# Norm statistics of two token blocks in one interleaved pass, with a retuned static schedule

## The chip, the cores and the metric

The kernel runs on one core of one Trainium2 chip. The metric is the device time of one execution in microseconds (us), lower is better. Every ratio below is of runs taken in the same rounds on the same chip.

## The reference, cut to what matters

```python
def _layernorm(x, axis=-1, eps=1e-05):
    m = jnp.mean(x, axis=axis, keepdims=True)
    v = jnp.var(x, axis=axis, keepdims=True)
    return (x - m) / jnp.sqrt(v + eps)

# x: (B, T, D) = (2, 4000, 144), 4 heads of 36
h = _layernorm(x); x = x + 0.5 * (_silu(h @ w_ff1a) @ w_ff1b)
h = _layernorm(x); q, k, v = split_heads(h @ w_qkv)          # cut
p = softmax(q @ k.T * 36 ** -0.5); x = x + (p @ v) @ w_o      # cut
h = _layernorm(x); ... # gated unit, depthwise convolution of 5 taps, silu, projection (cut)
h = _layernorm(x); x = x + 0.5 * (_silu(h @ w_ff2a) @ w_ff2b)
return _layernorm(x)
```

There are five layer norms over rows of 144 features. 8000 tokens are 64 blocks of 125 rows, so 320 block norms. The large part is the attention: 4000 x 4000 scores for each of 4 heads and 2 batches, each of which needs an exponential.

## The kernel before

The kernel is a program that writes a program. Python generators (one for each norm, projection, score tile) ask a scheduler for an engine; the scheduler keeps an assumed clock for each engine, takes the next step by assumed cost and by a *policy*, and the result is a fixed order of instructions for each engine with semaphore waits worked out from data dependences. Every instruction is issued from one helper line, so the profile gives all of them one line number (L169) and groups have to be told apart by tile.

The norm before, for `n` blocks of 125 rows (`c` is a chunk of four blocks):

```python
for j in range(n):                              # one block each: 144 columns -> 6 numbers
    op("dve", "bn_stats", ST[0:rows, u, j, :], X[0:rows, c * NB + b0 + j, :], ..., cost=0.21)
...
for j in range(n):                              # merge the even and odd halves -> mean, variance
    op("dve", "bn_aggr", MV[0:rows, u, j, :], ST[0:rows, u, j, :], ..., cost=0.08)
calm = mode["front"] or mode["tail"]
op("dve" if calm else "pool", "tensor_scalar", RS[.., 1, ..], MV[0:rows, u, 0:n, 1], LN_EPS, None, op0=ALU.add, ...)
op("pool", "tensor_tensor", RS[.., 0, ..], RS[.., 1, ..], NHALF[..], op=ALU.pow, ...)   # 1/sqrt
# middle: four POOL passes XN = (X - mean) * rstd, cost=XN_COST
# tail:   on ACT (activation Identity with scale and bias tiles, cost=c_act(D)) or on DVE
```

A score tile is 128 x 1000 exponentials. ACT does most of them. DVE does some by integer arithmetic: two reads of PSUM (128x500 each), then five passes over a 128x1000 tile of 16-bit numbers in SBUF. The policy decides which:

```python
BASE = dict(AHEAD=0.56, DSLACK=1.0, DGAP=3.5, OFREE=1, OBATCH=0, LATE=0.3, BMIN=2.2, SOON=3, LIVE=2, MAXQ=3, EARLY=1)
POLICY = {...}     # the same names, with one value for each of 18 phases of the attention (cut)

# a tile goes to DVE only if (cut)
live_dve[0] < now("LIVE") and early[0] < now("EARLY") and ... \
    and R.free["dve"] < R.free["pe"] + now("DSLACK") and R.free["pe"] > last_dve[0] + now("DGAP")
```

The other names set how the remaining matmuls and the post-processing (output projection, convolution, second feed-forward) are mixed in between.

The softmax here doesn't subtract the row's maximum and nothing guards it: scores larger than these inputs give would overflow.

Of the kernel before, what the change touches and what calls it, by code (L numbers as in the profile page):

```python
# [6 lines left out]
ALU = mybir.AluOpType  # L7
BF16 = mybir.dt.bfloat16
F16 = mybir.dt.float16
F32 = mybir.dt.float32  # L10
U16 = mybir.dt.uint16

D = 144
# [9 lines left out]
NB = 4  # L23
# [296 lines left out]
def bass_standalone__conformer_family_zipformer__speech_kernel(  # L320
# [28 lines left out]
    def sb(name, shape, dt=BF16):  # L349
        return nc.alloc_sbuf_tensor(name, [128] + list(shape), dt)  # L350
# [2 lines left out]
    NPT = 9  # L353
    NU = 5
    NAN = 5
    BASE = dict(AHEAD=0.56, DSLACK=1.0, DGAP=3.5, OFREE=1, OBATCH=0, LATE=0.3, BMIN=2.2, SOON=3, LIVE=2, MAXQ=3, EARLY=1)
    POLICY = {
        "AHEAD": [0.56, 0.56, 0.56, 0.56, 0.56, 0.75, 0.75, 0.56, 0.56, 0.56, 0.56, 0.56, 0.6, 0.56, 0.56, 0.56, 0.56, 0.56],
        "DGAP": [3.5, 3.5, 3.5, 3.5, 3.5, 3.5, 3.5, 3.5, 3.5, 3.5, 3.5, 3.5, 3.5, 3.5, 3.5, 3.5, 3.5, 4.0],
        "OFREE": [1, 1, 1, 1, 1, 1, 1, 1, 1, 1, 1, 1, 1, 1, 2, 1, 1, 1],  # L360
        "LATE": [0.3, 0.3, 0.6, 0.3, 0.3, 0.3, 0.3, 0.3, 0.3, 0.3, 0.3, 0.3, 0.3, 0.3, 0.3, 0.3, 0.3, 0.3],
        "BMIN": [2.2, 2.2, 2.2, 2.2, 2.2, 2.2, 2.2, 2.2, 2.2, 2.2, 2.2, 2.2, 2.2, 2.2, 2.2, 1.8, 1.8, 2.2],
        "MAXQ": [3, 3, 3, 3, 3, 3, 2, 2, 3, 3, 3, 3, 3, 3, 3, 3, 3, 3],
    }
    ROT = 0
    SPLIT = 0
# [17 lines left out]
    VG = 7  # L384
    X = sb("X", [NBLK, D])
    XN = sb("XN", [NXN, NB, D])
    ST = sb("ST", [NXN, NB, 6], F32)
    MV = sb("MV", [NXN, NB, 2], F32)
    RS = sb("RS", [NXN, 3, NB], F32)
    NHALF = sb("NHALF", [NB], F32)  # L390
    DUM = sb("DUM", [1], F32)
# [82 lines left out]
    for c in range(CPB, NCH):  # L474
        load_x("sp", c)

    op("pool", "memset", MV[:, :, :, :], 0.0, w=[("MV", u) for u in range(NXN)])
    op("act", "activation", DUM[:, :], NHALF[:, 0:1], ACT.Silu, bias=0.0, scale=1.0, r=["NHALF"], w=["DUM"], cost=1.6)
    for WE, WB, nm, eng in ((WE1, WB1, "W1", "dve"), (WE2, WB2, "W2", "pool")):
        op(eng, "memset", WE[0:HD, :, 0:64], 0.0, w=[(nm, "a", 2)], cost=0.15)  # L480
# [109 lines left out]
    def ln(c, bs, e=False):  # L590
        n, b0, rows = len(bs), bs[0], TB + e
        xe = ["XE"] * e
        u = yield need("dve", xnp)
        for j in range(n):
            op("dve", "bn_stats", ST[0:rows, u, j, :], X[0:rows, c * NB + b0 + j, :], r=[("X", c, b0 + j)] + xe,
               w=[("ST", u, j)], cost=0.21)
        yield need("dve", hold=mode["front"] or mode["tail"])
        for j in range(n):
            op("dve", "bn_aggr", MV[0:rows, u, j, :], ST[0:rows, u, j, :], r=[("ST", u, j)], w=[("MV", u)], cost=0.08)
        calm = mode["front"] or mode["tail"]  # L600
        if not calm:
            yield need("pool")
        op("dve" if calm else "pool", "tensor_scalar", RS[0:rows, u, 1, 0:n], MV[0:rows, u, 0:n, 1], LN_EPS, None,
           op0=ALU.add, r=[("MV", u)], w=[("VE", u)], cost=0.08 if calm else 0.25)
        if calm:
            yield need("pool")
        op("pool", "tensor_tensor", RS[0:rows, u, 0, 0:n], RS[0:rows, u, 1, 0:n], NHALF[0:rows, 0:n], op=ALU.pow,
           r=[("VE", u), "NHALF"], w=[("RS", u)], cost=0.7 if calm else POW_COST)
        if not calm:
            op("pool", "tensor_scalar", RS[0:rows, u, 2, 0:n], MV[0:rows, u, 0:n, 0], -1.0, None, op0=ALU.mult,  # L610
               r=[("MV", u)], w=[("NM", u)], cost=0.3)
            for j in range(n):
                op("pool", "tensor_scalar", XN[0:rows, u, j, :], X[0:rows, c * NB + b0 + j, :], RS[0:rows, u, 2, j:j + 1],
                   RS[0:rows, u, 0, j:j + 1], op0=ALU.add, op1=ALU.mult,
                   r=[("X", c, b0 + j), ("NM", u), ("RS", u)] + xe, w=[("XN", u)], cost=XN_COST, lat=XN_LAT)
        elif mode["tail"] and R.free["act"] + XSLACK < R.free["dve"]:
            yield need("dve", hold=True)
            op("dve", "scalar_tensor_tensor", out=RS[0:rows, u, 2, 0:n], in0=MV[0:rows, u, 0:n, 0], scalar=-1.0,
               in1=RS[0:rows, u, 0, 0:n], op0=ALU.mult, op1=ALU.mult, r=[("MV", u), ("RS", u)], w=[("NM", u)], cost=0.08)
            yield need("act")  # L620
            for j in range(n):
                op("act", "activation", XN[0:rows, u, j, :], X[0:rows, c * NB + b0 + j, :], ACT.Identity,
                   bias=RS[0:rows, u, 2, j:j + 1], scale=RS[0:rows, u, 0, j:j + 1],
                   r=[("X", c, b0 + j), ("NM", u), ("RS", u)] + xe, w=[("XN", u)], cost=c_act(D))
        else:
            yield need("dve")
            for j in range(n):
                op("dve", "tensor_scalar", XN[0:rows, u, j, :], X[0:rows, c * NB + b0 + j, :], MV[0:rows, u, j, 0:1],
                   RS[0:rows, u, 0, j:j + 1], op0=ALU.subtract, op1=ALU.mult,
                   r=[("X", c, b0 + j), ("MV", u), ("RS", u)] + xe, w=[("XN", u)], cost=0.231)  # L630
        return u

    XSLACK = 0.0
    XN_COST = 0.5
    XN_LAT = 0.5
    POW_COST = 1.1

    def ln_tr(c, s, bs, e=False):
        u = yield from ln(c, bs, e)
# [950 lines left out]
```

## Time and profile before

| | |
|---|---|
| time, median of the runs first taken | 954.24 us (954.09 to 955.26) |
| profiled span, mean granted clock | 953.0 us, 0.997 |
| last exponential tile done | 919.8 us |
| tiles on ACT and on DVE (128x1000) | 863 and 129 |

One place it did not look at is shown here. The first fence is PE's part of the timeline of the kernel before (start, duration, engine, operation, tiles, shape, count, and in brackets the idle time before it with what ended it); the second is the table of busy time by stretch (window, length, PE, PE weight load, DVE, ACT, POOL, then granted clock, DMA share, GB/s) around the same moment.

```profile
637.95 0.38 PE L169 MATMUL PS<-PT,VA 64*37 64x500 bf16 x4
640.37 0.39 PE L169 MATMUL PS<-U,DG 128*128 128x500 bf16 x1 [2.04 <-POOL U L169]
```

```profile
640.00:642.00 2.00, 1.63 (x11) 0.37 (x11) 1.51 (x3) 0.78 (x1) 0.31 (x2) 0.72 0.00 0
642.00:644.00 2.00, 2.00 (x16) 0.42 (x14) 1.00 (x2) 1.12 (x2) 0.00 (x0) 0.50 0.00 0
```

PE ran nothing for 2.04 us before a small POOL copy was done (tile U, the edges that the convolution borrows from its neighbour chunk; the copy itself stood behind four normalising passes that took 3.31 us), and then ran at half clock (0.50) for 3.4 us, from 640.87 to 644.28 us by windows of 0.1 us. The row of clock in tenths that the prediction read averages over 24 us a slice and hides it.

### The profile page before, as it was taken

Reading aid. Unit: us, or ns where it says so; the run is one execution under the profiler, and the core shown is the slowest. Engines: PE = TensorE matmul, PEld = TensorE weight load, DVE = VectorE, ACT = ScalarE, POOL = GpSimd, SP = SyncE. Lnnn points to the kernel's source line nnn. Section 1 sums busy time; section 2 is a strip of 40 time slices with the busy share of each in tenths; the row PEclk is TensorE's granted clock in tenths of the full one; section 3 lists DMA queues with packets and bytes.
Section 4 is the critical chain, followed back from the end, with each engine's and each line's share of the span. In section 5 each row is a group of like instructions: output and inputs, shape, how many; then the busy total and the mean of one; then the engine's idle time right before and its main releaser. Section 6 shows DMA issues by size and latency. Waiting matters only on the chain.

```text
span 953.0 us, 27142 instructions
## 1 busy us (share of the span) xinstructions
PE 902.5 (95%) x11491; PEld 407.6 (43%) x11491; DVE 861.2 (90%) x2291; ACT 904.9 (95%) x1150; POOL 308.3 (32%) x535
## 2 busy tenths in 40 slices
PE   8899999999999999999999999989998999999996
PEld 7543433443343444434444433433343344434456
DVE  7997797999999897899999999998989899999885
ACT  5799999999999999999999999999999999999984
POOL 4220024513134333333225421531234143431452
PEclk9999999999999999999999999999999999999999
DMA  4000000000000000000000000000000000000000
GB/s 120 23 2 2 2 2 2 1 2 1 2 2 1 2 2 2 7 1 2 2 8 7 3 8 2 13 1 2 2 14 1 1 9 1 14 1 3 7 8 20
DMA packets 7195, 7.34 MB, mean 8 GB/s; under 512 B 2372, under 2 KB 7074, under 8 KB 7074
## 3 DMA queue, kind: packets, MB, share of 16 engines
q1 hardware_dynamic: 5916, 5.14, 1.8%
q8 instruction: 90, 1.47, 0.7%
q10 hardware_dynamic: 1158, 0.48, 0.2%
q14 instruction: 31, 0.25, 0.1%
HBM read 3.31 MB, written 2.30 MB: 6 GB/s over the span
## 4 chain that ended last, share of the span: by engine, by line
ACT 43%; PE 34%; DVE 18%; POOL 3%; issue 1%; DMA 0%; POOLq 0%; DVEq 0%
ACT PT L169 37%; PE PS L169 34%; DVE PT L169 9%; ACT TH L169 5%; DVE HT L169 2%; POOL XN L169 2%; DVE ST L169 1%; POOL RS L169 1%; DVE XT L169 1%; DVE OTF L169 1%; DVE X L169 1%; DVE MV L169 1%; DVE AN L169 0%; DMA X<-in_x_dram 0%; DVE XN L169 0%
## 5 line engine op out<-in xcount | busy, mean ns | idle before, releaser
L169 ACT ACTIVATE PT<-PS 128x1000 bf16<-128x1000 f32 (+1 forms) x879 | 812.9, 1047 | 13.1 <-PE PS L169 11.3
L169 PE MATMUL PS<-QT,KT 64*64 64x500 bf16 x3968 | 412.5, 385 | 22.5 <-ACT PT L169 14.9
L169 PE MATMUL PS<-PT,VA 64*37 64x500 bf16 x3968 | 362.0, 375 | 4.5 <-DVE OTF L169 1.8
L169 PEld LDWEIGHTS PS<-QT,KT 64*64 64x64 bf16 x3968 | 123.7, 104 | 219.1 <-ACT PT L169 140.0
L169 DVE TENSOR_SCALAR PT<-PS 128x500 uint16<-128x500 f32 x258 | 172.4, 669 | 16.2 <-PE PS L169 15.1
L169 POOL TENSOR_SCALAR RS<-MV 125x4 f32<-125x4 f32 x118 | 39.8, 337 | 438.0 <-DVE MV L169 432.6
L169 DVE TENSOR_TENSOR PT<-PT 128x1000 uint16<-128x1000 uint16 (+1 forms) x258 | 174.0, 679 | 1.9
L169 PEld LDWEIGHTS PS<-PT,VA 64*37 64x37 bf16 x3968 | 114.6, 95 | 111.8 <-issue 30.5
L169 DVE TENSOR_SCALAR PT<-PT 128x1000 uint16<-128x1000 uint16 (+1 forms) x387 | 157.1, 422 | 2.3
L169 POOL TENSOR_SCALAR XN<-X,RS 125x144 bf16<-125x144 bf16 x236 | 153.9, 664 | 6.1
L169 POOL TENSOR_TENSOR RS<-RS,NHALF 125x4 f32<-125x4 f32 (+2 forms) x99 | 97.9, 994 | 118.2 <-DVE RS L169 113.3
L169 ACT ACTIVATE TH<-PS 128x500 bf16<-128x500 f32 (+2 forms) x208 | 111.6, 558 | 9.2 <-PE PS L169 8.4
L169 DVE SCALAR_TENSOR_TENSOR HT<-TH,PS 128x500 bf16<-128x500 bf16 (+1 forms) x145 | 87.0, 615 | 14.8 <-ACT TH L169 14.6
L169 DVE SCALAR_TENSOR_TENSOR X<-PS,X 125x288 bf16<-125x288 f32 x128 | 57.4, 452 | 23.0 <-PE PS L169 21.5
L169 DVE BATCH_NORM_STATS2 ST<-X 125x6 f32<-125x144 bf16 (+1 forms) x320 | 75.3, 294 | 1.3 <-DMA X<-in_x_dram 1.1
L169 PE MATMUL PS<-XT,WA 72*128 72x500 bf16 (+2 forms) x272 | 74.1, 366 | 2.0 <-ACT XTQ L169 0.9
L169 PE MATMUL PS<-WB,HT 128*125 128x144 bf16 (+1 forms) x640 | 52.6, 230 | 0.4 <-DVE HT L169 0.3
L169 PEld LDWEIGHTS PS<-WB,HT 128*125 128x125 bf16 (+1 forms) x640 | 44.1, 136 | 14.1 <-issue 6.3
L169 PE MATMUL PS<-IDENT,XN 125*72 125x125 bf16 x512 | 43.0, 222 | 5.3 <-POOL XN L169 1.8
L169 DVE COPY XT<-PS 72x1000 bf16<-72x1000 bf16 (+1 forms) x64 | 39.7, 623 | 5.9 <-PE PS L169 5.6
L169 PEld LDWEIGHTS PS<-IDENT,XN 125*72 125x72 bf16 x512 | 31.3, 112 | 25.9 <-issue 11.5
L169 POOL COPY U<-U 128x2 bf16<-128x2 bf16 (+1 forms) x54 | 13.8, 279 | 78.2 <-DVE U L169 78.2
(90 smaller groups left out, 636.0 us busy)
## 6 DMA issues: line engine op xcount, KB each, us to landing
X<-in_x_dram SPq DMA_DIRECT2D x16, 140.6 KB
out_dram<-XN SPq DMA_DIRECT2D x14, 140.6 KB
WA<-in_w_ff1a_dram ACTq DMA_DIRECT2D x1, 144.0 KB
WB<-in_w_ff1b_dram ACTq DMA_DIRECT2D x1, 144.0 KB, 2.5
WA<-in_w_ff2a_dram SPq DMA_DIRECT2D x1, 144.0 KB
WB<-in_w_ff2b_dram SPq DMA_DIRECT2D x1, 144.0 KB
out_dram<-XN SPq DMA_DIRECT2D x2, 70.3 KB
out_dram<-XN SPq DMA_DIRECT2D x1, 139.5 KB
```

The lines of the kernel that those rows point to most:

```text
L169: ins = getattr(eng, o.name)(*o.a, **o.k)
```

## The change

Intent: the instruction that takes statistics gives six numbers a row (125x6 from 125x144 in the trace of the kernel before), and a second one merges them to two (125x2 from 125x6). The change takes the six to be those of the even and of the odd columns, separately. If two blocks are read alternately, x0[0], y0[0], x0[1], y0[1], ..., the even half *is* one block and the odd half the other. One instruction of 288 columns then replaces two of 144 and both merges. Of a half's three numbers the change takes one as the mean and one as the sum of squared deviations, so the add of epsilon also divides by 144. At the same time the policy was retuned and the assumed POOL costs were raised. The core of the diff, cuts marked:

```diff
-    BASE = dict(AHEAD=0.56, DSLACK=1.0, DGAP=3.5, OFREE=1, OBATCH=0, LATE=0.3, BMIN=2.2, SOON=3, LIVE=2, MAXQ=3, EARLY=1)
+    BASE = dict(AHEAD=0.56, DSLACK=0.2, DGAP=4.0, OFREE=1, OBATCH=1, LATE=0.3, BMIN=2.0, SOON=2, LIVE=3, MAXQ=3, EARLY=2)
     POLICY = {   # (all lists by phase replaced; cut)
-    ST = sb("ST", [NXN, NB, 6], F32)
-    MV = sb("MV", [NXN, NB, 2], F32)
+    ST = sb("ST", [NXN, NB, 3], F32)
-    op("pool", "memset", MV[:, :, :, :], 0.0, w=[("MV", u) for u in range(NXN)])
-        for j in range(n):
-            op("dve", "bn_stats", ST[0:rows, u, j, :], X[0:rows, c * NB + b0 + j, :], r=[("X", c, b0 + j)] + xe,
-               w=[("ST", u, j)], cost=0.21)
-        yield need("dve", hold=mode["front"] or mode["tail"])
-        for j in range(n):
-            op("dve", "bn_aggr", MV[0:rows, u, j, :], ST[0:rows, u, j, :], r=[("ST", u, j)], w=[("MV", u)], cost=0.08)
+        for j in range(0, n, 2):
+            op("dve", "bn_stats", ST[0:rows, u, j:j + 2, :].rearrange("p i k -> p (i k)"),
+               xv(c, range(b0 + j, b0 + j + 2), rows).rearrange("p i d -> p d i"),
+               r=[("X", c, b0 + j), ("X", c, b0 + j + 1)] + xe, w=[("MV", u)], cost=0.365)
-        op("dve" if calm else "pool", "tensor_scalar", RS[0:rows, u, 1, 0:n], MV[0:rows, u, 0:n, 1], LN_EPS, None,
-           op0=ALU.add, r=[("MV", u)], w=[("VE", u)], cost=0.08 if calm else 0.25)
+        op("dve" if calm else "pool", "tensor_scalar", RS[0:rows, u, 1, 0:n], ST[0:rows, u, 0:n, 2], 1.0 / D, LN_EPS,
+           op0=ALU.mult, op1=ALU.add, r=[("MV", u)], w=[("VE", u)], cost=0.08 if calm else 0.25)
   (readers of MV[.., 0] read ST[.., 1] instead; cut)
-    XN_COST = 0.5
-    XN_LAT = 0.5
-    POW_COST = 1.1
+    XN_COST = 0.65
+    XN_LAT = 0.1
+    POW_COST = 1.22
```

More of the change, by code (lines that the diff above doesn't have):

```diff
@@ L355, in bass_standalone__conformer_family_zipformer__speech_kernel @@
     NAN = 5
-    BASE = dict(AHEAD=0.56, DSLACK=1.0, DGAP=3.5, OFREE=1, OBATCH=0, LATE=0.3, BMIN=2.2, SOON=3, LIVE=2, MAXQ=3, EARLY=1)
+    BASE = dict(AHEAD=0.56, DSLACK=0.2, DGAP=4.0, OFREE=1, OBATCH=1, LATE=0.3, BMIN=2.0, SOON=2, LIVE=3, MAXQ=3, EARLY=2)
     POLICY = {
-        "AHEAD": [0.56, 0.56, 0.56, 0.56, 0.56, 0.75, 0.75, 0.56, 0.56, 0.56, 0.56, 0.56, 0.6, 0.56, 0.56, 0.56, 0.56, 0.56],
-        "DGAP": [3.5, 3.5, 3.5, 3.5, 3.5, 3.5, 3.5, 3.5, 3.5, 3.5, 3.5, 3.5, 3.5, 3.5, 3.5, 3.5, 3.5, 4.0],
-        "OFREE": [1, 1, 1, 1, 1, 1, 1, 1, 1, 1, 1, 1, 1, 1, 2, 1, 1, 1],
-        "LATE": [0.3, 0.3, 0.6, 0.3, 0.3, 0.3, 0.3, 0.3, 0.3, 0.3, 0.3, 0.3, 0.3, 0.3, 0.3, 0.3, 0.3, 0.3],
-        "BMIN": [2.2, 2.2, 2.2, 2.2, 2.2, 2.2, 2.2, 2.2, 2.2, 2.2, 2.2, 2.2, 2.2, 2.2, 2.2, 1.8, 1.8, 2.2],
-        "MAXQ": [3, 3, 3, 3, 3, 3, 2, 2, 3, 3, 3, 3, 3, 3, 3, 3, 3, 3],
+        "DSLACK": [0.2, 0.2, 0.2, 0.2, 0.2, 0.2, 0.2, 1.0, 1.0, 0.6, 0.2, 0.2, 0.2, 0.2, 0.2, 0.2, 0.2, 0.2],
+        "DGAP": [4.0, 4.0, 4.0, 4.0, 4.0, 4.0, 4.0, 4.0, 4.0, 4.0, 4.0, 4.0, 4.5, 4.5, 4.0, 4.0, 4.0, 4.0],
+        "OFREE": [1, 1, 1, 1, 1, 1, 1, 1, 1, 1, 1, 3, 1, 3, 0, 0, 0, 1],
+        "OBATCH": [1, 1, 1, 1, 1, 1, 1, 1, 1, 1, 1, 1, 1, 0, 1, 1, 1, 2],
+        "BMIN": [2.0, 2.0, 2.0, 2.0, 1.8, 1.8, 1.8, 2.0, 2.0, 1.6, 2.0, 3.5, 2.0, 2.0, 2.0, 2.0, 2.0, 1.8],
+        "SOON": [2, 2, 2, 2, 2, 2, 2, 2, 2, 2, 2, 2, 2, 2, 2, 2, 5, 3],
+        "LIVE": [3, 2, 2, 2, 3, 3, 3, 3, 3, 2, 2, 3, 3, 3, 2, 3, 3, 3],
+        "MAXQ": [3, 3, 3, 3, 3, 3, 3, 3, 2, 2, 2, 2, 2, 3, 3, 3, 3, 3],
+        "EARLY": [2, 2, 2, 2, 2, 2, 2, 1, 1, 1, 1, 1, 1, 2, 2, 2, 2, 2],
     }
@@ L593, in ln @@
         u = yield need("dve", xnp)
-        for j in range(n):
-            op("dve", "bn_stats", ST[0:rows, u, j, :], X[0:rows, c * NB + b0 + j, :], r=[("X", c, b0 + j)] + xe,
-               w=[("ST", u, j)], cost=0.21)
-        yield need("dve", hold=mode["front"] or mode["tail"])
-        for j in range(n):
-            op("dve", "bn_aggr", MV[0:rows, u, j, :], ST[0:rows, u, j, :], r=[("ST", u, j)], w=[("MV", u)], cost=0.08)
+        for j in range(0, n, 2):
+            op("dve", "bn_stats", ST[0:rows, u, j:j + 2, :].rearrange("p i k -> p (i k)"),
+               xv(c, range(b0 + j, b0 + j + 2), rows).rearrange("p i d -> p d i"),
+               r=[("X", c, b0 + j), ("X", c, b0 + j + 1)] + xe, w=[("MV", u)], cost=0.365)
         calm = mode["front"] or mode["tail"]
-        if not calm:
-            yield need("pool")
-        op("dve" if calm else "pool", "tensor_scalar", RS[0:rows, u, 1, 0:n], MV[0:rows, u, 0:n, 1], LN_EPS, None,
-           op0=ALU.add, r=[("MV", u)], w=[("VE", u)], cost=0.08 if calm else 0.25)
+        yield need("dve" if calm else "pool", hold=calm)
+        op("dve" if calm else "pool", "tensor_scalar", RS[0:rows, u, 1, 0:n], ST[0:rows, u, 0:n, 2], 1.0 / D, LN_EPS,
+           op0=ALU.mult, op1=ALU.add, r=[("MV", u)], w=[("VE", u)], cost=0.08 if calm else 0.25)
         if calm:
@@ L609, in ln @@
         if not calm:
-            op("pool", "tensor_scalar", RS[0:rows, u, 2, 0:n], MV[0:rows, u, 0:n, 0], -1.0, None, op0=ALU.mult,
+            op("pool", "tensor_scalar", RS[0:rows, u, 2, 0:n], ST[0:rows, u, 0:n, 1], -1.0, None, op0=ALU.mult,
                r=[("MV", u)], w=[("NM", u)], cost=0.3)
@@ L617, in ln @@
             yield need("dve", hold=True)
-            op("dve", "scalar_tensor_tensor", out=RS[0:rows, u, 2, 0:n], in0=MV[0:rows, u, 0:n, 0], scalar=-1.0,
+            op("dve", "scalar_tensor_tensor", out=RS[0:rows, u, 2, 0:n], in0=ST[0:rows, u, 0:n, 1], scalar=-1.0,
                in1=RS[0:rows, u, 0, 0:n], op0=ALU.mult, op1=ALU.mult, r=[("MV", u), ("RS", u)], w=[("NM", u)], cost=0.08)
@@ L627, in ln @@
             for j in range(n):
-                op("dve", "tensor_scalar", XN[0:rows, u, j, :], X[0:rows, c * NB + b0 + j, :], MV[0:rows, u, j, 0:1],
+                op("dve", "tensor_scalar", XN[0:rows, u, j, :], X[0:rows, c * NB + b0 + j, :], ST[0:rows, u, j, 1:2],
                    RS[0:rows, u, 0, j:j + 1], op0=ALU.subtract, op1=ALU.mult,
```

## The prediction

> **What bounds the kernel now.** I began with the first page of the profile, for the load of each engine, then its row of granted clock, which reads 9 tenths or more in every slice, so no throttle needs explaining.
>
> ```profile
> PE 902.5 (95%) x11491; PEld 407.6 (43%) x11491; DVE 861.2 (90%) x2291; ACT 904.9 (95%) x1150; POOL 308.3 (32%) x535
> ```
>
> Three engines are nearly full at once, so a share over the whole span settles nothing, and I asked for busy time in three stretches: the front from 10 to 65 us, where the first batch is being projected and few exponentials can run; the long middle; and the tail after 920 us.
>
> ```profile
> 10.00:65.00 55.00, 51.52 (x651) 29.69 (x652) 53.02 (x218) 45.08 (x74) 15.98 (x23) 1.00 0.15 43
> 65.00:920.00 855.00, 817.59 (x10441) 349.16 (x10434) 781.58 (x1959) 839.63 (x1037) 277.27 (x473) 1.00 0.01 4
> 920.00:953.00 33.00, 25.55 (x328) 21.42 (x328) 20.32 (x89) 16.67 (x36) 9.93 (x20) 0.98 0.07 19
> ```
>
> The columns after the length are PE, PE weight load, DVE, ACT and POOL. In the front DVE is busy 53.0 of 55 us (96%). In the middle ACT is busy 839.6 of 855 (98%) and DVE 91%. In the tail no engine is full: it is a chain of latencies. So three different things bound the three stretches. The groups of instructions say what the middle is made of:
>
> ```profile
> L169 ACT ACTIVATE PT<-PS 128x1000 bf16<-128x1000 f32 x863 | 805.5, 1054 | 13.0 <-PE PS L169 11.3 <-DVE PT L169 0.2
> ...
> L169 DVE TENSOR_SCALAR PT<-PS 128x500 uint16<-128x500 f32 x258 | 172.4, 669 | 16.2 <-PE PS L169 15.1
> ...
> L169 DVE BATCH_NORM_STATS2 ST<-X 125x6 f32<-125x144 bf16 x316 | 74.3, 294 | 1.2 <-DMA X<-in_x_dram 1.1
> ...
> L169 DVE BATCH_NORM_AGGREGATE MV<-ST 125x2 f32<-125x6 f32 x316 | 31.0, 155 | 0.0
> ```
>
> ACT does 863 full score tiles, DVE does another 129 (258 halves) by an integer trick. That number is a choice of the scheduler which writes the static program: it sends a tile to DVE when DVE has room. So the two engines share one pool of work, and **DVE time that is freed in the middle pays only if more tiles go from ACT to DVE.** The list of waits says where PE stands:
>
> ```profile
> PEld PS L169 <- ACT PT L169: 157.7, 380, 1.2
> ```
>
> From 65 to 920 us PE's weight loads wait 158 us for ACT to read a score bank, while ACT's exponentials wait only 10 us for PE. PE is close behind, but ACT is the one being waited for.
>
> [...] statistics of 144 columns start 0.208 us apart and PSUM reads of 500 columns 0.58 us apart, (580 - 208) / 356 = 1.045 ns a column; the fixed part is 208 - 150 = 58 ns here. [...] four normalising passes on POOL took 1.97 us at 170.3 and 4.30 us at 174.2, the second beside DVE's PT passes.
>
> **The change, part by part.** What a DVE instruction costs is the distance between starts, for consecutive ones overlap in the records:
>
> ```profile
> 168.38 0.91 DVE L169 BATCH_NORM_STATS2 ST<-X 125x6 f32<-125x144 bf16 x4
> 169.21 0.66 DVE L169 COPY XT<-PS 72x1000 bf16<-72x1000 bf16 x1
> ...
> 170.37 0.37 DVE L169 BATCH_NORM_AGGREGATE MV<-ST 125x2 f32<-125x6 f32 x4
> 170.66 0.64 DVE L169 TENSOR_SCALAR PT<-PS 128x500 uint16<-128x500 f32 x1
> ```
>
> Four statistics take 169.21 - 168.38 = 0.83 us, four merges 0.29 us: 1.12 us per norm of four blocks. After: two statistics of 288 columns, [...] and no merge. Saved: 0.40 us per four blocks. There are 320 / 4 = 80 such norms: 32 us of DVE, 480 fewer instructions (640 become 160). The division of the second moment by the width goes into the existing add of epsilon as its second operation: free. The memset of MV (133 ns on POOL at 2 us) goes; nothing waits for it.
>
> Where the 80 fall, from the instructions on ST in the same stretches (94, 498 and 40, half of them statistics, over four): 11.75 in the front, 62.25 in the middle, 5 in the tail, one before 10 us.
>
> Front: 11.75 x 0.40 = 4.7 us off an engine busy 96%. PE (94%) is close behind and carries 47% of the chain there, so I count 3 us.
>
> Middle: 62.25 x 0.40 = 24.9 us of DVE, worth nothing directly. A tile on DVE costs 2 x 0.58 (PSUM reads) + 3 x 0.33 + 2 x 0.585 (the PT passes, start to start) = 3.32 us. On ACT it costs 0.894 us (twelve tiles in 10.88 us, one lasting 1.054). If DVE stays 91% full, each moved tile also shortens the window by 0.894 us, so the number moved is 24.9 / (3.32 + 0.91 x 0.894) = 6.0, worth 6.0 x 0.894 = 5.4 us.
>
> Tail: two of its norms show on the last chain, at 938.4 and 946.5 us. The first spends 0.84 us in four statistics and 0.16 us in two merges before its epsilon; now one long statistic per half. About 0.5 us there, 0.2 at the last, some for those before: 1 us.
>
> The rest is retuning. The scheduler's assumed POOL costs rise (0.5 to 0.65 us a normalising pass, trace mean 0.664; 1.1 to 1.22 for the power, trace 1.172), so its order fits the chip better; more DVE tiles may be alive at once (LIVE and EARLY), while their least distance grows (3.5 to 4.0) and DSLACK falls. PE's direct waits for POOL are only about 5 us in all, so I allow 1 us of gain.
>
> Sum: 3 + 5.4 + 1 + 1 = 10.4 us; 954.2 - 10.4 = 943.8, about 944.
>
> **Rivals.** First, *the alternating read is slow.* [...] For it: no such read in this trace. Against: [...] the author's assumed 0.365, close to my 0.358. I give it one in ten.
>
> Second, *freed DVE time stays idle.* DVE already idles 73 us in the middle, where its waits are for PE and ACT, not for work of its own[...]. If no tile moves, only front and tail remain: about 950. For it: PE at 96% in the middle and the more careful DSLACK. Against: the retuned policy was evidently searched for this load.
>
> Third, *the freed time is used better than I count.* If the new policy also fills a quarter of those 73 us, that is 5 more tiles, 4 to 5 us: about 939. Beyond that PE is in the way: at 817.6 us busy, the middle cannot shrink to under 2% of the whole without PE being full.
>
> Fourth, *POOL.* [...] At 32% busy, and released mostly by DVE (its wait for MV sums to 433 us), it has room; perhaps 1 us.
>
> **Range and chances.** The first rival sets the tail above, the second the 950 side, the third the low end: 935.5 to 953 should hold eight times in ten. Faster by over 2% means under 935.2, nearly twice my sum: 0.10. Slower by 2% needs over 973[...]: 0.03. Within 2%: 0.87.
>
> **What would show it right or wrong.** The statistics should be 160 of 125x288 lasting 294 + 150 = about 444 ns[...]. No merge rows. Exponential tiles on ACT should fall from 863 to about 857 and the halves on DVE rise from 258 to about 270; unchanged counts mean the second rival, over 280 the third. ACT should still be about 98% busy in the middle and DVE about 91%; if ACT waits for PE by far more than the present 10 us, PE has taken over and my exchange sum fails. The front should reach its steady run of exponentials about 3 us sooner.

The sum came to 3 + 5.4 + 1 + 1 = 10.4 us, and its four terms stand; passages that rested on what no trace or run of this case shows are cut. One of them is the price of the new statistic, on which the terms of front, middle and tail rest. With the slope that the prediction took from the trace, 1.045 ns a column, it is the same estimate: 0.208 us + 144 x 1.045 ns = 0.358 us an instruction, 0.72 us for two, and 1.12 - 0.72 = 0.40 us saved per four blocks. That the second operation in the add of epsilon is free can be read from the two traces: the instruction takes 337 ns on POOL before and 343 after (125x4), 169 and 159 on DVE (125x2).

## More of the kernel before

`c_act(n)` is `n / 1200 + 0.051`, so the scheduler counts 0.171 us for a normalising pass of 144 columns on ACT.

## The result, and the profile after

The kernel after took 950.63 us in the median of four runs (948.65 to 951.54), the kernel before 954.2. The ratio is 0.9957, with a 95% interval of 0.9938 to 0.9976: 3.6 us saved by the medians, where 10 were forecast. (A ratio here is taken from the runs of both kernels in the same rounds; it is not quite the ratio of the medians.) It lies in the forecast range and in the class of "within 2%", but the gain is a third of the sum.

The profiled span fell from 953.0 to 949.6 us. First the engine totals of the kernel after (busy time, share of the span, instructions):

```profile
PE 892.5 (94%) x11433; PEld 406.3 (43%) x11433; DVE 855.9 (90%) x1881; ACT 899.8 (95%) x1153; POOL 303.1 (32%) x524
```

Then its busy time in three stretches, cut where its last score tile ended (columns as before: PE, weight load, DVE, ACT, POOL, clock, DMA share, GB/s):

```profile
10.00:65.00 55.00, 53.06 (x681) 30.61 (x683) 51.62 (x159) 45.27 (x76) 16.78 (x24) 1.00 0.15 44
65.00:911.70 846.70, 804.95 (x10346) 346.23 (x10338) 776.78 (x1627) 827.29 (x1019) 270.79 (x463) 1.00 0.01 4
911.70:949.60 37.90, 27.10 (x333) 22.70 (x330) 21.57 (x73) 23.38 (x55) 10.50 (x20) 0.92 0.06 16
```

The attention ends at 911.7 instead of 919.8 us, 8.1 us sooner. What comes after it takes 37.9 us; before it took 953.0 - 919.8 = 33.2 us. So 8.1 us were won and 4.7 given back. (The clock of 0.92 in the last row is no cause: by 5 us stretches it is 1.00 until 941.7, and 0.67 only after PE's last matmul.)

The groups of instructions of the kernel after (engine, operation, output<-input, shapes, count, busy us, mean ns, idle before them):

```profile
L169 ACT ACTIVATE PT<-PS 128x1000 bf16<-128x1000 f32 x853 | 795.8, 1054 | 13.2 <-PE PS L169 11.4
...
L169 DVE TENSOR_SCALAR PT<-PS 128x500 uint16<-128x500 f32 x278 | 186.0, 670 | 15.4 <-PE PS L169 14.7
...
L169 DVE BATCH_NORM_STATS2 ST<-X 125x6 f32<-125x288 bf16 x158 | 64.7, 447 | 1.3 <-DMA X<-in_x_dram 1.2
```

The statistics last 447 ns (444 forecast), the merges are gone, ten tiles moved from ACT to DVE (863 to 853, 258 to 278 halves), and ACT's waits for PE did not grow. As counts, the exchange went as described, a little further; what it was worth is another question (e2 below). Two things in this trace were not in the forecast.

**The tail.** ACT's normalising passes, all of which lie in the tail, in the kernel before and then after:

```profile
L169 ACT ACTIVATE XN<-X,RS 125x144 bf16<-125x144 bf16 (+1 forms) x8 | 3.5, 504 | 6.2 <-DVE RS L169 6.2
```

```profile
L169 ACT ACTIVATE XN<-X,RS 125x144 bf16<-125x144 bf16 (+1 forms) x22 | 9.5, 496 | 5.3 <-DVE RS L169 5.3
```

The end of the kernel after is a run of eight of them, here in its timeline:

```profile
942.58 3.29 ACT L169 ACTIVATE XN<-X,RS 125x144 bf16<-125x144 bf16 x8 [0.90 <-DVE RS L169]
```

From start to start one costs (3.29 - 0.50) / 7 = 0.40 us; the scheduler counts 0.171. Also more work was left to the tail: 14 residual adds followed the last score tile, 10 before.

**A stall of PE, and the clock.** PE, POOL and DVE in the timeline of the kernel after:

```profile
264.18 0.59 PE L169 MATMUL PS<-PT,VA 64*37 64x500 bf16 x8
266.98 0.39 PE L169 MATMUL PS<-U,DG 128*128 128x500 bf16 x1 [2.22 <-POOL U L169]
...
264.52 2.66 POOL L169 COPY U<-U 80x1 bf16<-80x1 bf16 x3 [2.03 <-DVE U L169]
...
264.97 1.25 DVE L169 TENSOR_TENSOR PT<-PT 128x1000 uint16<-128x1000 uint16 x2
266.14 0.74 DVE L169 TENSOR_SCALAR PT<-PT 128x1000 uint16<-128x1000 uint16 x2
```

and the busy time of the same kernel in stretches of 2 us:

```profile
266.00:268.00 2.00, 1.02 (x7) 0.34 (x7) 0.88 (x3) 0.20 (x1) 1.17 (x3) 0.88 0.00 0
268.00:270.00 2.00, 2.00 (x10) 0.56 (x8) 0.00 (x0) 1.81 (x2) 0.00 (x0) 0.50 0.00 0
...
272.00:274.00 2.00, 2.00 (x21) 1.06 (x23) 0.87 (x2) 0.75 (x2) 0.00 (x0) 0.50 0.00 0
274.00:276.00 2.00, 2.00 (x28) 0.59 (x21) 0.18 (x1) 0.72 (x2) 0.00 (x0) 0.91 0.04 8
```

Three small copies take 2.66 us while DVE runs its passes over the 16-bit tiles; PE waits 2.22 us for them; then the granted clock is 0.50 for 6.8 us (267.53 to 274.35 by windows of 0.1 us), and ACT, which lives on PE's scores, is busy 0.75 of 2 us from 272 on.

### The profile page after: what moved, and what is told of

Read it like the earlier page. It is cut to its first block, busy times and chain, and to the rows that moved or that the text cites. A ratio compares the mean times of both kernels' runs of the same rounds, so it can differ in the third digit from the quotient of the medians.

```text
span 949.6 us, 26625 instructions
## 1 busy us (share of the span) xinstructions
PE 892.5 (94%) x11433; PEld 406.3 (43%) x11433; DVE 855.9 (90%) x1881; ACT 899.8 (95%) x1153; POOL 303.1 (32%) x524
## 4 chain that ended last, share of the span: by engine, by line
ACT 55%; PE 34%; DVE 8%; issue 1%; DMA 0%; POOL 0%; DVEq 0%
ACT PT L169 49%; PE PS L169 34%; ACT TH L169 5%; DVE PT L169 4%; DVE HT L169 1%; DVE ST L169 1%; ACT XN L169 1%; DVE X L169 1%; DMA X<-in_x_dram 0%; DVE XT L169 0%; DVE OTF L169 0%; DVE U L169 0%; ACT HT L169 0%; POOL U L169 0%; DVE XN L169 0%
## 5 line engine op out<-in xcount | busy, mean ns | idle before, releaser
L169 ACT ACTIVATE PT<-PS 128x1000 bf16<-128x1000 f32 (+1 forms) x869 | 804.0, 1046 | 16.1 <-PE PS L169 14.2
L169 DVE TENSOR_SCALAR PT<-PS 128x500 uint16<-128x500 f32 x278 | 186.0, 670 | 15.4 <-PE PS L169 14.7
L169 DVE TENSOR_TENSOR PT<-PT 128x1000 f16<-128x1000 f16 (+1 forms) x278 | 187.6, 680 | 2.3
L169 POOL TENSOR_SCALAR RS<-ST 125x4 f32<-125x4 f32 x114 | 39.1, 343 | 427.3 <-DVE ST L169 421.7
L169 DVE TENSOR_SCALAR PT<-PT 128x1000 uint16<-128x1000 uint16 (+1 forms) x417 | 167.4, 417 | 2.6
L169 POOL TENSOR_SCALAR XN<-X,RS 125x144 bf16<-125x144 bf16 x228 | 143.9, 643 | 5.9
L169 ACT ACTIVATE TH<-PS 128x500 bf16<-128x500 f32 (+2 forms) x201 | 108.4, 562 | 8.4 <-PE PS L169 7.9
L169 DVE SCALAR_TENSOR_TENSOR HT<-TH,PS 128x500 bf16<-128x500 bf16 (+1 forms) x140 | 83.8, 615 | 12.9 <-ACT TH L169 12.7
L169 DVE BATCH_NORM_STATS2 ST<-X 125x6 f32<-125x288 bf16 (+1 forms) x160 | 65.5, 447 | 1.4 <-DMA X<-in_x_dram 1.2
L169 POOL COPY U<-U 128x2 bf16<-128x2 bf16 (+1 forms) x54 | 17.1, 343 | 103.4 <-DVE U L169 103.4
```

The lines of the kernel that those rows point to most:

```text
L169: ins = getattr(eng, o.name)(*o.a, **o.k)
```

## The experiments

The theory after reading the traces: the exchange is right, and its gain was lost to (a) stalls of PE behind POOL passes that DVE slows, with the half clock after them, and (b) a longer tail. The rivals: the retuned policy and not the statistics makes the difference, so that the time is a draw from a wide spread of schedules; the freed DVE time is worth little because the schedule is not DVE-bound; the new statistic disturbs POOL itself. In each quoted expectation, theories are named as they stood at that time.

All runs but the last row agree with the reference. Only e4 differs from the kernel before by 2% or more. The ratios are of the same rounds; differences in us between runs of different rounds are of medians, and the medians of the kernel before in the five sets of rounds were 954.2, 954.3, 955.1, 954.3 and 954.4 us, so that nothing under 1 us should be read from them. The medians also mix runs of different mean granted clock: the four runs of the kernel after took 951.5, 951.4, 949.8 and 948.7 us at clocks of 0.995, 0.993, 0.996 and 0.998.

| run | what it is | median us (range) | ratio |
|---|---|---|---|
| e1_stats_alone | new statistics, old policy and costs | 957.47 (955.84 to 960.52) | 1.0024 |
| e2_retune_alone | old statistics, new policy and costs | 949.18 (948.96 to 953.53) | 0.9953 |
| f1_flat_policy_old | before, lists by phase emptied | 966.49 (966.35 to 968.09) | 1.0125 |
| f2_flat_policy_new | same with new statistics | 964.16 (958.76 to 964.36) | 1.0082 |
| e3_before_order | before's exact order, statistics swapped in place | 947.94 (947.06 to 948.68) | 0.9929 |
| e4_after_order_split | after's order, statistics split in place | 980.50 (980.20 to 982.05) | 1.0274 |
| e5_after_fill | after, PE's stall filled | 948.54 (948.38 to 948.73) | 0.9932 |
| e6_before_fill | before, filler in the wrong place | 956.97 (956.17 to 957.17) | 1.0019 |
| e7_before_fill_right | before, PE's stall filled | 952.77 (952.68 to 952.84) | 0.9986 |
| e8_stats_alone_fill | e1, three stalls filled | 955.27 (953.83 to 955.47) | 1.0009 |
| e10_tail_cost | e5, ACT's normalising pass costed at 0.41 | 946.00 (945.90 to 946.25) | 0.9908 |
| e9_other_policy | new statistics, a plain other policy | 940.82 (940.75 to 940.91) | 0.9860 |
| e11_other_policy_tail | e9 with the cost of e10 | 941.25 (941.04 to 941.38) | 0.9858 |
| e12_other_policy_old | e9's policy, old statistics | 955.65 (955.48 to 955.66) | 1.0009 |
| e13_best_old | old statistics, policy picked for them | 956.85 (954.86 to 959.13) | 1.0023 |
| m1_pool_and_clock | a kernel of its own | 463.92 (one run) | - |

### The two halves of the change alone: e1, e2

e1 is the kernel after with the old policy lists and old POOL costs put back; e2 is the kernel before with the new ones.

```diff
 e1, against after (lists by phase likewise; cut)
-    BASE = dict(AHEAD=0.56, DSLACK=0.2, DGAP=4.0, OFREE=1, OBATCH=1, LATE=0.3, BMIN=2.0, SOON=2, LIVE=3, MAXQ=3, EARLY=2)
+    BASE = dict(AHEAD=0.56, DSLACK=1.0, DGAP=3.5, OFREE=1, OBATCH=0, LATE=0.3, BMIN=2.2, SOON=3, LIVE=2, MAXQ=3, EARLY=1)
-    XN_COST = 0.65
-    XN_LAT = 0.1
-    POW_COST = 1.22
+    XN_COST = 0.5
+    XN_LAT = 0.5
+    POW_COST = 1.1
 e2, against before: the same edit the other way round
```

> The paired statistics of the change, with the scheduler's policy and assumed POOL costs of the kernel before. Theory A (the merge is worth what was counted for DVE, and the retuned policy is what came out less well): this run is as fast as the full change or faster, 945 to 950 us, with about 140 score tiles on DVE. Theory B (the retuning is what made the change pay, and the freed DVE time stays idle without it): 951 to 954 us and about 130 tiles on DVE. Theory C (PE is the limit and every gain is given back at the end): about 950 us, whatever the policy.

> The new policy and the new assumed POOL costs, with the separate statistics and merges of the kernel before. Theory A: the policy is a draw of its own and can go either way by some 5 us, 946 to 956 us, with about 130 score tiles on DVE. Theory B: about 950 us, nearly all of the change's gain. Theory C: about 954 us, as nothing was taken off any engine.

The statistics with the old policy were *slower* than before, 957.5 us, although 140 tiles ran on DVE; nothing written down had expected that. The retuning with the old statistics gave 949.2 us, as much as the whole change. The two parts do not add: +3.2 and -5.0 make -1.8, the whole is -3.6. In the trace of e1 PE stands three times behind POOL's normalising passes, 2.8, 1.9 and 1.8 us. The first, in the timelines of PE's weight loads, POOL and DVE:

```profile
136.42 0.47 PEld L169 LDWEIGHTS PS<-IDENT,XN 125*72 125x72 bf16 x8 [2.76 <-POOL XN L169]
...
130.98 5.39 POOL L169 TENSOR_SCALAR XN<-X,RS 125x144 bf16<-125x144 bf16 x4
...
132.27 2.44 DVE L169 TENSOR_TENSOR PT<-PT 128x1000 f16<-128x1000 f16 x4
```

Four passes took 5.39 us where the scheduler had assumed 2.0; the clock was 0.50 for 13.6 us, from about 137.5 to 151.1 us.

The trace of e2 bears on the largest term of the forecast. Its middle, cut at its last score tile (columns as before):

```profile
65.00:912.15 847.15, 806.10 (x10381) 345.61 (x10380) 776.55 (x1945) 833.77 (x1028) 271.99 (x463) 1.00 0.01 4
```

With the old statistics, 861 full tiles on ACT and 131 on DVE, that is only two tiles moved, its attention ends at 912.2 us: 7.7 us sooner than in the kernel before, and almost where the kernel after ends it (911.7). Its tail of 35.4 us has the same 14 residual adds as that of the kernel after. So an early end of the attention does not show that moved tiles made it.

### How much of this is the draw of a policy: f1, f2

Both kernels with the lists by phase emptied, so that only `BASE` of before counts; f2 has before's assumed POOL costs.

```diff
-    POLICY = { ... }
+    POLICY = {}
```

> The kernel before with its per-phase policy lists emptied, so that one plain policy (its own base values) holds throughout; separate statistics. To be compared with f2, which differs from it in the statistics alone. Theory A (at equal policy the merge is worth what I counted, and the gain was lost because the two tuned policies are not equally good draws): 956 to 960 us. Rival (schedules hardly matter): 954 us.

> The same plain policy as f1, with the paired statistics. Theory A: 8 to 12 us faster than f1, 946 to 950 us (up to 5 us more if a PE stall behind POOL halves the clock somewhere). Rival (the merge is worth about 4 us whatever the policy): 3 to 5 us faster than f1.

Untuned, the old statistics make 966.5 and the new ones 964.2 us, with 124 and 140 tiles on DVE; both are slower than anything expected of them. f2 moved sixteen tiles more than f1 and gained 2.3 us: it has five gaps of PE behind POOL of 1.7 to 2.8 us, and a mean clock of 0.986 to 0.987 in three runs; the fourth run, at 0.994, took 958.8. So before's lists by phase, a matter of order alone, are worth 12.3 us with the old statistics (966.5 against 954.2) and 6.7 with the new (964.2 against e1), as much as or more than the whole gain forecast for the middle.

### No tile moved: e3, e4

e3 keeps the order of the kernel before to the instruction. The scheduler still charges the old statistics and merges; they are dropped before waits are worked out, and the paired statistic stands where the first of its pair stood.

```diff
 (cut to the core)
+            o = op("dve", "bn_stats", ST[.., g:g + 2, :], xv(c, range(b0 + g, b0 + g + 2), rows).rearrange("p i d -> p d i"), ..., cost=0.21)
+            if j % 2:
+                o.ghost = pair[-1]
-            op("dve", "bn_aggr", MV[0:rows, u, j, :], ST[0:rows, u, j, :], r=[("ST", u, j)], w=[("MV", u)], cost=0.08)
+            op("dve", "bn_aggr", r=[("ST", u, j)], w=[("MV", u)], cost=0.08).ghost = pair[j // 2]
     def finish(self):
+        self.ops = [o for o in self.ops if o.ghost is None]
```

e4 is the opposite: the order of the kernel after, each paired statistic split into two plain ones and two merges on the spot, with the same total charge.

```diff
-            op("dve", "bn_stats", ..., w=[("MV", u)], cost=0.365)
+            for k in (j, j + 1):
+                op("dve", "bn_stats", ST[0:rows, u, k, :], X[0:rows, c * NB + b0 + k, :], ..., cost=0.1825, lat=-0.036)
+            for k in (j, j + 1):
+                op("dve", "bn_aggr", MV[0:rows, u, k, :], ST[0:rows, u, k, :], ..., cost=0.0)
```

> The kernel before in its own instruction order on every engine, with only the separate statistics and merges replaced by the paired ones in place (the scheduler still decides with the old costs). No tile moves from ACT to DVE. Theory A: freed DVE time without moved tiles is worth little: 950 to 953 us, the gain in the front and in the tail, ACT's 863 full tiles unchanged. Theory C: 953 to 954. If DVE was the limit after all: 940 or less.

> The changed kernel in its own instruction order on every engine, with each paired statistics instruction replaced in place by two separate ones and two merges, so DVE has about 30 us more work than the order was made for. Theory A (DVE time is what the order was made with, and there is little slack): 960 to 975 us. Theory C (PE is the limit, DVE has room): 951 to 956 us.

e3 took 947.9 us, 6.3 less than before, *less than the kernel after* and less than the 950 to 953 expected, with not one tile moved (863 on ACT still). DVE's busy time fell from 861.2 to 832.6 us. Its stretches, cut at its last score tile, and the clock after its stall:

```profile
10.00:65.00 55.00, 52.42 (x668) 29.74 (x667) 48.70 (x151) 46.44 (x74) 16.73 (x24) 1.00 0.15 43
65.00:914.80 849.80, 815.19 (x10414) 348.67 (x10410) 759.38 (x1580) 836.32 (x1035) 260.49 (x474) 1.00 0.01 4
914.80:946.70 31.90, 25.44 (x332) 21.58 (x328) 18.26 (x59) 16.83 (x36) 8.52 (x18) 0.96 0.06 17
...
638.00:640.00 2.00, 2.00 (x16) 0.55 (x16) 1.19 (x3) 1.69 (x2) 0.00 (x0) 0.50 0.00 0
```

By 65 us ACT had done 26 full tiles, against 24 in the kernel before: 2 x 0.894 = 1.8 us won in the front. The last tile ended 5.0 us sooner in all and the tail took 31.9 instead of 33.2 us, 1.3 less. The stall was shorter here (1.23 us between PE's matmuls, 2.04 before), but the half clock after it is there as in the kernel before, from 636.9 to 640.3 us (0.50 in the stretch shown). That leaves 5.0 - 1.8 = 3.2 us for the middle, some 0.8 of it at that stall. (This split is worked out from one trace, and is an estimate.)

e4 took 980.5 us, above the 960 to 975 expected: 32 us more DVE work by the forecast's own costs (80 norms x 0.40) made 30 us more time. In the order of the kernel after, nearly all of the added DVE time shows in the span. The same work is thus worth 6 us taken out of one order and 30 put into the other. That this is because the second order has filled the freed time with tiles is argued, not shown: e4 also makes every norm's chain longer, and has one more stretch of half clock (3.4 us at 741 us; the mean clock of its profiled run is 0.991, that of the kernel after 0.993).

### POOL beside DVE, and the clock after a gap: m1

A kernel of its own. Part 1 runs four normalising passes on POOL, each time beside a run of one kind of DVE instruction. Part 2 lets PE wait for DVE for 0.7 to 3.1 us between bursts of 70 matmuls.

```python
for kind, runs in (("none", (0,)), ("bn1", (12, 12)), ("bn", (8, 8)), ("ps", (6, 6)), ("ts", (2, 4, 8, 8)), ("tt", (2, 4, 8, 8))):
    for m in runs:
        op("dve", "tensor_copy", G[:, 0:8], G[:, 8:16], ..., w=["go"])
        for _ in range(4):
            xn()            # POOL: XN = (X + a) * b, 125x144 bf16
        for k in range(m):
            dve(kind, k)    # single or paired statistic, PSUM read, one-input or two-input pass over 1000 f16
```

> A kernel of its own, with a wrong result on purpose. Part 1: four normalising passes on POOL, alone and beside runs of one kind of DVE instruction each. Theory D: a pass takes about 0.46 us alone and beside statistics or PSUM reads, and well over 1 us, up to the length of the whole run, beside the 16-bit passes of a score tile (1000 columns, SBUF to SBUF). Rival (POOL slows beside any DVE work, the paired statistics with their alternating read among them): 1 us beside the statistics too. Part 2: PE busy for about 15 us, then idle for 0.8 to 3.2 us, then busy again, three times each. Theory D: full clock after gaps up to about 1.6 us, 0.50 for several us after gaps of 2.4 us and more.

Part 1, four passes on POOL in its timeline: alone, beside paired statistics, and beside two-input SBUF passes (the last shown as its first two of four); with the DVE runs beside the second and third (of the last, five of eight):

```profile
22.40 1.78 POOL L169 TENSOR_SCALAR XN<-X,RS 125x144 bf16<-125x144 bf16 x4 [0.31 <-DVE G L169]
27.98 1.78 POOL L169 TENSOR_SCALAR XN<-X,RS 125x144 bf16<-125x144 bf16 x4 [1.01 <-DVE G L169]
61.43 3.70 POOL L169 TENSOR_SCALAR XN<-X,RS 125x144 bf16<-125x144 bf16 x2 [0.31 <-DVE G L169]
...
27.79 2.98 DVE L169 BATCH_NORM_STATS2 ST<-X 125x6 f32<-125x288 bf16 x8
61.23 3.13 DVE L169 TENSOR_TENSOR A<-A 128x1000 f16<-128x1000 f16 x5
```

1.78 us alone, and 1.78 beside either kind of statistic or beside PSUM reads. Beside two, four and eight one-input SBUF passes 2.12, 2.53 and 3.43; beside two-input ones 2.65, 3.57 and 5.51. So in this run the statistics, old or new, did not slow POOL (1.78 us); passes like those of DVE's score tiles did, up to threefold (5.51): a microsecond of two-input passes delayed POOL by about 0.7 us ((5.51 - 1.78) / 5.01), one of one-input passes by about 0.5. The same run answers the first rival of the prediction: eight paired statistics in 2.98 us start (2.98 - 0.447) / 7 = 0.362 us apart, and single ones 0.21. The estimate of 0.358 us counted the columns alone, so the alternating read cost next to nothing.

Part 2, PE's timeline and the busy time around one burst:

```profile
143.08 15.28 PE L169 MATMUL PS<-IDENT 128*128 128x512 bf16 x70 [1.93 <-DVE G L169]
160.70 16.97 PE L169 MATMUL PS<-IDENT 128*128 128x512 bf16 x70 [2.33 <-DVE G L169]
180.40 15.28 PE L169 MATMUL PS<-IDENT 128*128 128x512 bf16 x70 [2.73 <-DVE G L169]
```

```profile
160.00:162.00 2.00, 1.30 (x5) 0.58 (x6) 0.64 (x1) 0.00 (x0) 0.85 0.00 0
162.00:164.00 2.00, 2.00 (x6) 0.72 (x5) 0.00 (x0) 0.00 (x0) 0.50 0.00 0
```

(This kernel has no ACT column.) Of the bursts that PE's timeline shows in full from 120 to 240 us, those after gaps of 0.73, 1.53, 1.93 and 2.73 us took 15.28 us, and those after 2.33 and 3.14 us took 16.97. By the count over the whole trace none of twelve gaps of 0.73 to 1.93 us was followed by half clock, and five of nine of 2.33, 2.73 and 3.13 us were; the mean clock of the run was 0.982. How long a half clock lasts can be read from rows like those above: 2 us at 0.85 are 1.4 us at 1.00 and 0.6 at 0.50, so the one shown begins at 161.4 us; it fills the next 2 us, and of those from 164 to 166 us, at 0.80, it takes 0.8: 3.4 us in all. In the larger kernels it lasted 3.4 us (before), 6.8 (after) and 13.6 (the longest in e1). So the length of a stop alone does not tell whether half clock follows it: the gap of 2.73 us shown here escaped where the shorter of 2.33 did not, and in e3 half clock followed a stop of 1.23 us. Why was not shown.

### Filling the stall: e5, e6, e7, e8

If the half clock after a stall costs time, matmuls that only keep PE busy while it waits should win it back. e5 puts 38 of them (results thrown away) before the convolution that stalls in the kernel after. The inserted code, in the matmul part of the convolution:

```diff
+        for _ in range(38 if c in (0,) else 0):
+            op("pe", "matmul", PSV[:, bk, 0:128], lhsT=IDENT[:, :], rhs=IDENT[:, :], start=True, stop=True, r=["ID"],
+               w=[("ps", bk)], cost=0.0, kind="f")
```

e6 has the same in the kernel before for another chunk; e7 counts the convolutions in order of time and puts 35 before the eighth; e8 puts 39, 23 and 21 before the three waiting transposes of e1:

```diff
 e6, against before (the operation is the same as in e5)
+        for _ in range(38 if c in (7,) else 0):
 e7, against before
+        for _ in range({7: 35}.get(seen[0], 0)):
 ...
+        seen[0] += 1
 e8, against e1, in the transposes of a normalised tile
+        for _ in range({128: 39, 416: 23, 440: 21}.get(seen[1], 0) if rk[0] == "XN" else 0):
 ...
+        seen[1] += 2 * n * (rk[0] == "XN")
```

> The changed kernel in its own order, with 38 dummy matmuls (some 2.1 us) put on PE before the first convolution, where PE stood idle for 2.7 us waiting for the slow halo copy on POOL and the granted clock then fell to 0.50 for some 7 us. The dummies write the bank that the convolution overwrites. Theory D (a PE stall of over 2 us behind POOL halves the clock, and that ate most of the missing gain): no clock dip near 267 us, mean clock 0.997 or more in every run, median 946 to 948 us, 3 to 5 us faster than the changed kernel. Rival (the clock dip is chance or costs nothing, the gain was given back in the tail): 950 to 951 us, as the changed kernel.

> The kernel before in its own order, with the same 38 dummy matmuls before its eighth convolution, where it has a PE gap of 2.5 us behind POOL at 640 us and a dip of the clock. Theory D: 951 to 952.5 us, 2 to 3 us faster than the kernel before, so that without dips the change would be worth 5 to 6 us. Rival: 954 us.

> The kernel before in its own order with 35 dummy matmuls at the place of its PE gap at 640 us (the earlier try put them before another convolution). Theory D: no dip, 951 to 953 us, 1.5 to 3 us faster than the kernel before. Rival: 954 to 957 us.

> The run with the paired statistics under the old policy, in its own order, with dummy matmuls before the three transposes that waited 2.8, 1.9 and 1.8 us for POOL. The stalls themselves stay. Theory D: mean clock 0.997, 949 to 952 us instead of 957.5. Rival (its slowness is not the clock's): 956 to 958 us.

In e5 the filler stands in PE's timeline, and the stretches keep full clock:

```profile
264.80 2.29 PE L169 MATMUL PS<-IDENT 128*128 128x128 bf16 x38
```

```profile
266.00:268.00 2.00, 2.00 (x27) 1.24 (x24) 0.98 (x3) 0.14 (x1) 1.27 (x3) 1.00 0.00 0
268.00:270.00 2.00, 2.00 (x20) 0.75 (x18) 0.00 (x0) 2.00 (x3) 0.00 (x0) 1.00 0.00 0
```

It took 948.5 us (946 to 948 expected), 2.1 less than the kernel after, and its five runs lie within 0.35 us of each other where those of the kernel after spread over 2.9; the fastest of those, at a mean clock of 0.998, took 948.65, as long as e5. The convolution itself did not start sooner (267.08 against 266.98): what was won is the clock, not the wait. e7 did the same for the kernel before and won 1.5 us. e6 was a mistake of placement: chunk 7 is not the eighth in time, the filler fell at about 711 us, where PE was not idle, and the gap of 2.5 us with its half clock stayed. It serves as the control: filler where PE is busy does not help but costs 1.9 us against the kernel before of the same rounds (957.0 against 955.1). With both kernels rid of the half clock, the change is worth 952.8 - 948.5 = 4.2 us by the medians, 5 by the ratios.

e8 was a miss: 949 to 952 was expected of it, 955.3 measured, only 2.2 us less than e1. Its trace shows that it did not get rid of the half clock, and its mean clock was 0.993 to 0.995 (e5: 0.997 to 0.998). The attention ends at 916.8 us instead of 923.3, 6.5 us sooner (e1's profiled run is its slowest), but then the clock is 0.50 from 930.4 to 940.7 us, in the tail, while PE still works; e1, at a mean clock of 0.986 in the profiled run, has 6.8 us of it there. What of e1's loss would be left at full clock was not measured.

### What ACT's pass costs in the tail: e10, e11

e10 changes one number in e5: what the scheduler counts for a normalising pass on ACT. The chip's work is of the same kind; only the choice between ACT and DVE in the tail changes.

```diff
-                   r=[("X", c, b0 + j), ("NM", u), ("RS", u)] + xe, w=[("XN", u)], cost=c_act(D))
+                   r=[("X", c, b0 + j), ("NM", u), ("RS", u)] + xe, w=[("XN", u)], cost=0.41)
```

e11 is the same edit in e9 (below).

> The changed kernel with the filled stall (as e5, 948.5 us), and the scheduler's assumed cost of a normalising pass on ACT raised from 0.171 to the 0.41 us that the trace shows start to start; this branch is used in the tail alone, so everything before the tail keeps its order. Theory E (the tail is long because it sends too many passes to ACT at a wrongly assumed cost): fewer than 22 such passes, the tail 2 to 4 us shorter, 945 to 946.5 us. Rival (the tail is long because one block more of post-processing is left for it): 948 to 949 us.

> The policy of e9 (940.8 us) with the same correction of the assumed ACT cost. Theory E: 939 to 940.5 us (it has 16 such passes). Rival: 941 us or slower.

In e10 ACT's group of normalising passes (by form) is down from 22 to 10:

```profile
L169 ACT ACTIVATE XN<-X,RS 125x144 bf16<-125x144 bf16 x10 | 4.5, 505 | 4.8 <-DVE RS L169 4.8
```

and the time from 948.5 to 946.0 us, the tail from 37.9 to about 35 us. The mis-costed pass was thus about 2.5 us of the loss (2.3 by the ratios, 2.9 by the tails of the two traces). e11, the same correction on e9, changed 16 passes to 14 and nothing in the time (941.25 against 940.82): that tail had not leaned on ACT.

The traces have 496 to 505 ns for such a pass and 0.40 us from start to start, against the 0.171 us that the scheduler counts.

### Another policy: e9, e12, e13

Three hundred random flat policies were ranked by the scheduler's own planned end, for the new statistics and for the old, and the best of each went to the chip: e9 (new statistics, no lists by phase) and e13 (old). e12 is e9's policy with the old statistics and before's assumed POOL costs.

```diff
 e9, against after
-    BASE = dict(AHEAD=0.56, DSLACK=0.2, DGAP=4.0, OFREE=1, OBATCH=1, LATE=0.3, BMIN=2.0, SOON=2, LIVE=3, MAXQ=3, EARLY=2)
-    POLICY = { ... }
+    BASE = dict(AHEAD=0.56, DSLACK=1.0, DGAP=3.75, OFREE=1, OBATCH=1, LATE=0.4, BMIN=2.4, SOON=3, LIVE=2, MAXQ=3, EARLY=2)
+    POLICY = {}
 e12, against before: the same BASE and POLICY
 e13, against e12
+    BASE = dict(AHEAD=0.56, DSLACK=0.4, DGAP=3.75, OFREE=1, OBATCH=0, LATE=0.2, BMIN=2.0, SOON=3, LIVE=3, MAXQ=3, EARLY=1)
```

> The paired statistics with another plain policy, the best by the scheduler's own planned end out of 300 drawn at random (6 us shorter in plan than the changed kernel). Theory A (only the draw of the policy stood in the way): 941 to 945 us. Theory D (a plan with less slack is met by more stalls behind POOL, which the plan does not know): 946 to 955 us, with gaps of PE behind POOL over 1.4 us.

> The policy of e9 with the separate statistics and merges of the kernel before. If the statistics made the gain: 950 to 955 us. If the policy made it: 941 to 946 us.

> The separate statistics with the policy that was best for them among the same 300 drawn at random, by the planned end. If the merge is worth what I counted (some 9 us) once both have a well-chosen policy: 946 to 951 us. If choosing the policy is all: 941 to 944 us.

e9 took 940.8 us, 1.4% under the kernel before and the fastest of all; its four runs lie within 0.2 us. Its middle and its tail:

```profile
65.00:906.70 841.70, 803.57 (x10361) 345.71 (x10354) 770.43 (x1617) 827.64 (x1022) 275.37 (x469) 1.00 0.01 4
906.70:939.10 32.40, 25.25 (x300) 20.54 (x298) 20.82 (x69) 20.86 (x46) 8.14 (x10) 0.95 0.06 19
```

Against the kernel after, 5.0 us come from the middle (2.1 of which e5 had put down to the half clock) and 5.5 from the tail. It has 137 tiles on DVE, two fewer than the kernel after, and no gap of PE behind POOL over 1.4 us, though its longest normalising pass on POOL is 4.44 us: PE did not wait that long for it. The gain therefore does not come from more tiles; what stands next to what is the likely source, which no run here takes apart.

With e9's policy the old statistics take 955.7 us, so there the statistics are worth 14.8 us: more than the forecast's 9.4 for front, middle and tail. But that policy was picked for the new statistics, and e12 has the old assumed POOL costs as well. The best found for the old ones, e13, came out no better (956.9, with gaps of 2.6, 1.7 and 1.7 us behind POOL and a clock of 0.991 in the profiled run), where 946 to 951 was expected; its two runs at a clock of 0.997 took 954.9, as long as before's searched lists. Best against best of what ran here (940.8 against e2's 949.2), the two kinds of statistics differ by 8.4 us; as both are the best of few and unequal draws, this is no measure of the statistics alone.

## Why the prediction was wrong, point by point

**What bounds the kernel, and the statistics.** Right. 447 ns against 444, no merges, 0.362 us from start to start for the alternating read where 0.358 was estimated (m1), and the slow-read rival is out.

**Middle: tiles are exchanged between DVE and ACT, 5.4 us.** The tiles moved as described, ten instead of six, ACT stayed at 98% and DVE at 92% in the middle, and the attention ended 8.1 us sooner, against 3 + 5.4 = 8.4 forecast for front and middle. That agreement is luck: the stall at 267 us took 2 us out of it, the front gave nothing, more post-processing was left for later, and e2 ends its attention 7.7 us sooner with two tiles moved. Under the new order and at full clock, old against new statistics are e2 against e5: 912.2 - 908.9 = 3.3 us with eight tiles moved, where the forecast's 0.894 us a tile would make 7.2. So that a moved tile is worth its whole time on ACT was not shown, and this pair speaks against it.

**Front: 3 us.** This step failed. By 65 us the kernel after had done 24 full tiles on ACT, as before; DVE's busy time there fell from 53.0 to 51.6 us and PE's rose from 51.5 to 53.1 of 55. e3 shows that the freed time can be used (26 tiles by 65 us, 1.8 us); in the new order it was not. Why not was not tested: the fuller PE is a hint, not a proof. (The 47% that the prediction gave for PE's share of the chain is of the window from 0 to 60 us; from 10 to 65 it is 58%.)

**Tail: 1 us.** This is the term that failed most: -1 forecast, +4.7 measured. The gain that was summed is real (1.3 us in e3, where the order is kept); but the tail was taken as fixed apart from it, and the new order changed it, with 14 residual adds left in place of 10 and 22 ACT passes in place of 8, each costing more than twice what the scheduler counts. e10 shows about 2.5 us of it to be that cost. That the adds make up the rest was not tested. The cost could be read before: four such passes in 1.70 us at 940.9 in the kernel before are 0.40 us apart.

**Fourth rival, POOL: "perhaps 1 us".** The cause is one that the prediction saw in the trace of the kernel before (four passes on POOL in 1.97 us, and in 4.30 beside DVE's PT passes), and m1 bears it out; the size was wrong, for two reasons. A slowed POOL pass costs nothing that shows until PE reaches the instruction that needs it (e9, with a pass of 4.44 us, has no gap of PE behind POOL over 1.4 us), and then PE runs nothing else (2.22 us at 267 us in the kernel after); and the clock was 0.50 after such a stop, for 3.4 us in the kernel before and 6.8 in the kernel after. e5 shows 2.1 us in the kernel after for the clock alone, e7 1.5 in the kernel before. The 5 us of waits for POOL were those of the matmuls alone (2.0 + 1.8 + 1.5, the last at the start); the rows of the weight loads list 9.6 us, and their column of the longest wait shows the stall at 640 us, 2.5 us in one piece. m1 adds that passes with two SBUF inputs slowed POOL most (5.51 us for its four passes, 3.43 beside as many with one input), a difference that the prediction did not make.

**Retuning: 1 us.** This step failed too, in kind. With the old statistics it gave 5.0 us (e2), and the statistics under the old policy lost 3.2 (e1): the parts do not add. Between policies, the same new statistics ran from 940.8 to 964.2 us and the old from 949.2 to 966.5.

**Freed DVE time in the middle is "worth nothing directly".** Wrong, as far as e3 tells: of 6.3 us without a moved tile, 1.8 lie in the front, 1.3 in the tail, and some 3.2 in the middle.

**The sum.** e10, in which the half clock of the stall and the cost in the tail are mended, takes 946.0 us; the forecast was 944. In its trace the attention ends at 909.0 us, 10.8 sooner than before (9.4 were forecast for front, middle and retuning together), and the tail is 35.0 us, still 1.8 longer and not 1 shorter: what is missing lies in the tail. So the attention ended as early as forecast or earlier, though by e2 most of that came with the new order and not with the moved tiles; of this gain a part was given back in the tail and in one stall; and the forecast's fault was to add freed work to a schedule as though the rest of it stayed where it was.

**What stays open.** What e1 would take at full clock. What a moved tile is worth. Why the front of the kernel after uses none of its freed DVE time, and why its tail is long beyond the cost of ACT's passes. What decides whether half clock follows a stop of PE, and for how long. And what the best policy for either kind of statistics is: e9 was the best of 300, by the plan and not by the chip.

## What to carry to other kernels

When a change frees time in a program whose order is computed, first swap the work in place with the order kept (as e3), and only then retune: the draw of the schedule here was larger than the effect sought, and one sample of it says little about the change. In such a program look for the few places where an engine stands for some 2 us behind a slow helper, since the stop and the clock after it can cost more than the sum of waits suggests (the clock alone 2.1 us here in the kernel after, 1.5 in the kernel before), and check every assumed cost against start-to-start times in the trace, above all on the last chain.
